# Attention with a mixture of experts: scores three tiles ahead, exponentials two, sum copies on VectorE

## The chip, the cores and the metric

The kernel runs on one core of a Trainium2 chip. The metric is the device time of one execution in microseconds (us); lower is better. Several executions are timed and their median counts. One more execution was recorded by the hardware profiler; the rows below are from it.

## What is computed

Attention over pooled queries (2 batches, 8 heads, 1152 positions, head size 64), then four experts, each a two-layer network with ReLU, weighted by a gate:

```python
q_pool = q.reshape(B, H, S // 2, 2, D).mean(axis=3)
scores = scale * np.matmul(q_pool, k.transpose(0, 1, 3, 2))
scores = scores - np.max(scores, axis=-1, keepdims=True)
attn = np.exp(scores)
attn = attn / (np.sum(attn, axis=-1, keepdims=True) + 1e-09)
attn_out = np.matmul(attn, v)                 # [2, 8, 576, 64]
x = attn_out.transpose(0, 2, 1, 3).reshape(B * S, H * D)
p = domain_probs / (domain_probs.sum(-1, keepdims=True) + 1e-09)
for e in range(E):
    h = np.maximum(x @ w1[e], 0.0)
    out += p[:, e:e + 1] * (h @ w2[e])
```

## The kernel before

The order of the instructions of each engine is the order in which the program is written; no scheduler changes it. The engines run side by side and wait for one another by semaphores, and each takes its own instructions strictly in order.

**The attention part** goes over 8 pairs of heads, n = 0 to 7 (pairs 0 to 3 are batch 0). Each pair has 9 tiles, i = 0 to 8, of 128 rows of scores by 1152 keys; tile number g = 9n + i. A tile goes through these steps:

- `scores(g)`: TensorE (PE) writes the scores into the PSUM tile `spt` (three banks; its pool `ps_s` has a single buffer). `S_rows` (L334, L338) does so for most tiles, `S_chunk` (L324) for tile 8 and for pair 0. Then `neg_scores(g)` on VectorE (DVE, L341) copies them to one of three SBUF buffers `sx`, scaled and negated, with the minimum of each row.
- `exps(g)`: ScalarE (ACT, L347) replaces `sx` by the exponentials and sums each row.
- `T_chunk(g, c)`: PE transposes `sx` in 18 pieces (L202) into two PSUM tiles `pt` (pool `ps_t`, two buffers); ACT copies the first to `aT` (L363), DVE the second (L361).
- `pv_part(g)`: a part of the product of `aT` with the values, in PSUM tile `po` (L376). Tiles 0 to 3 of a pair form group 0 (256 columns), whose product is made in tiles 4 to 8; tiles 4 to 8 form group 1 (320 columns), whose product is made in tiles 0 to 3 of the next pair. `PVCUT` cuts it: three key blocks in tile 0, two in tiles 1 to 7, one in tile 8. The last part calls `finish`: DVE multiplies `po` by the inverse sums `rb` (L416), and the result is split into a high and a low part for the expert products, in batch 0 by ACT (L419) and POOL (GpSimd, L420), in batch 1 mostly by POOL.
- `inv_sums` (DVE L385, L386, then a POOL copy into `spread`, L387) and `spread_sums` (PE transposes `spread` into a `pt` buffer called `pr`, L394 and L396, and ACT copies it to `rb`, L397 and L400) make `rb`.

The loop over g issues for tile g: `T_chunk(g)`, `exps(g+1)`, `pv_part(g)`, then in some tiles `spread_sums` or a preparation step, at last `scores(g+2)`.

**Preparation of a later pair.** `prep_q` and `prep_k` (table `PREP`) make the operands of the next pair out of loaded q and k. `prep_q(n)`: 12 transposes on PE into a `pt` buffer called `pq`, an ACT copy to `raw` (L280), splits into high and low parts on POOL (`pool_split`, L209 and L210), DMAs issued by SP that stack the halves, and at its end `join_k(1)`, a POOL copy (L262) that `prep_k(n, 1)` transposes. `prep_k(n, c)`: 8 transposes `pk`, a copy to `raw` (DVE for c = 1, ACT for c = 2), POOL splits, stacking DMAs. `add_q` and `join_k(0)`, on POOL, form their inputs from the loads.

**The expert part** follows at about 256 us and takes the rest: 16 units of products. Its first products (`chx`, L135) are put into tiles 7 and 8 of the last pair; between them ACT copies `chx` to `UT["m1"]` (L543).

The PSUM pools:

```python
ps_t = ctx.enter_context(tc.tile_pool(name="ps_t", bufs=2, space=PSUM))
ps_s = ctx.enter_context(tc.tile_pool(name="ps_s", bufs=1, space=PSUM))
ps_o = ctx.enter_context(tc.tile_pool(name="ps_o", bufs=1, space=PSUM))
```

Of the kernel before, what the change touches and what calls it, by code (L numbers as in the profile page):

```python
# [8 lines left out]
F32 = mybir.dt.float32  # L9
F32R = mybir.dt.float32r  # L10
AF = mybir.ActivationFunctionType
ALU = mybir.AluOpType
# [5 lines left out]
def attention_moe_kernel(ctx, tc, q, k, v, probs, w1, w2, out):  # L18
    nc = tc.nc
# [4 lines left out]
    HALF = 64  # L24
    NPAIR = H // 2
    KT = S // P
    NQT = 9
# [13 lines left out]
    CW = HT // 2  # L41
# [101 lines left out]
    with ExitStack() as actx:  # L143
# [246 lines left out]
        def spread_sums(n, grp):  # L390
            pt = ps_t.tile([P, 2, 512], F32, tag="t", name="pr")[:, 0]
            r = rs[n % 2][:, 4 * grp:]
            for j in range(2):
                nc.tensor.transpose(pt[:, j * P:(j + 1) * P], spread[:, j * P:(j + 1) * P], ident)  # L394
            if grp:
                nc.tensor.transpose(pt[:, 2 * P:3 * P], r[:, 4:5].to_broadcast([P, P]), ident)  # L396
            nc.scalar.activation(rb[grp][:, :256], pt[:, :256], AF.Copy)  # L397
            if grp:
                for a, h in enumerate(ROWS):
                    nc.scalar.activation(rb[1][h, 256:], pt[h, 256 + a * HALF:256 + (a + 1) * HALF], AF.Copy)  # L400

        def split_x(op, kt, c, src, eng):
            hi, lo = xop(op, 0, kt)[:, c], xop(op, 1, kt)[:, c]
# [6 lines left out]
        def finish(n, grp, po):  # L410
            b, hp = pairs[n]
            w, kt = GW[grp], hp % 2
            c = slice(256 * grp, 256 * grp + w)
            c1 = slice(HT + 256 * grp, HT + 256 * grp + w)
            x = xr[:, hp, c1 if b else c]
            nc.vector.tensor_tensor(x, po[:, :w], rb[grp], ALU.mult)  # L416
            if b == 0:
                op = "A12" if hp > 1 else "A11"
                nc.scalar.activation(xop(op, 0, kt)[:, c], x, AF.Copy)  # L419
                nc.gpsimd.tensor_tensor(xop(op, 1, kt)[:, c], x, xop(op, 0, kt)[:, c].bitcast(F32), ALU.subtract)  # L420
                return
            a11, a12, a21 = xr[:, kt, c], xr[:, kt + 2, c], xr[:, kt, c1]
            if hp < 2:
                nc.gpsimd.tensor_tensor(a11, a11, x, ALU.subtract)
                if hp == 0:
                    split_x("S3", 0, c, a11, nc.gpsimd)
                return
            eng = nc.vector if hp == 3 else nc.gpsimd
            eng.tensor_tensor(a11, x, a11, ALU.subtract)
            todo = [("S2", a11), ("S1", a21), ("A22", x), ("S4", a12)]  # L430
            if eng is nc.gpsimd:
                eng.tensor_tensor(a21, a21, x, ALU.add)
                eng.tensor_tensor(a12, a12, a11, ALU.subtract)
                for op, src in todo:
                    split_x(op, kt, c, src, eng)
                return
            hi, lo = split_parts(todo[0], kt, c)
            hi()
            eng.tensor_tensor(a21, a21, x, ALU.add)
            eng.tensor_tensor(a12, a12, a11, ALU.subtract)  # L440
            rest = [split_parts(t, kt, c) for t in todo[1:]]
            late.append([lo] + [r[1] for r in rest])
            late.append([r[0] for r in rest])
            if grp == 0:
                for fn in late.pop() + late.pop():
                    fn()
# [44 lines left out]
        for fn in ev:  # L491
# [7 lines left out]

        PVCUT = {0: (1, -1, 0, 3), 1: (1, -1, 3, 5), 2: (1, -1, 5, 7), 3: (1, -1, 7, 9),  # L500
                 4: (0, 0, 0, 2), 5: (0, 0, 2, 4), 6: (0, 0, 4, 6), 7: (0, 0, 6, 8), 8: (0, 0, 8, 9)}
        SPREAD = {7: (0, 0), 1: (-1, 1)}
        PREP = {0: [(prep_q,)], 2: [(prep_k, 1)], 4: [(prep_k, 2)]}
        PREP0 = {3: [(prep_q,)], 4: [(prep_k, 1)], 5: [(prep_k, 2)]}

        def pv_part(g):
# [19 lines left out]
        for g in range(NTL):  # L526
# [2 lines left out]
                load_kv(vn[(n + 1) % 2], v, n + 1)  # L529
            if i == 6 and n + 2 < NP:  # L530
                add_q(nc.gpsimd)
            if i == 8 and n + 2 < NP:
                join_k(0)
            if i == 2 and n + 2 < NP:
                load_q(n + 2)
            for c in range(2):
                T_chunk(g, c)
            if g + 1 < NTL:
                exps(g + 1)
            if i == 8:  # L540
                inv_sums(n, 1)
            if g == NTL - 1:
                nc.scalar.activation(UT["m1"], chx[:, :2, :CW], AF.Copy)  # L543
            pv_part(g)
            if i in SPREAD and n + SPREAD[i][0] >= 0:
                spread_sums(n + SPREAD[i][0], SPREAD[i][1])
            if g == 0:
# [1 line left out]
            if n + 1 < NP:  # L549
                for fn, *args in (PREP if n else PREP0).get(i, []):  # L550
                    fn(n + 1, *args)
                if i == (4 if n else 5) and n + 2 < NP:
                    load_kv(kn, k, n + 2)
            elif i == 7:
                chx = ps_s.tile([P, 3, 512], F32, tag="s", name="chx")
                for kt in range(2):
                    product(0, 0, kt, chx, True)
            elif i == 8:
                for kt in range(2):
                    product(0, 2, kt, chx, False)  # L560
            scores(g + 2)
            if g == 0:
                stack_k0()
                add_q(nc.gpsimd)
                join_k(0)
                join_k(1)
            if i == 3:
                inv_sums(n, 0)
            if (n, i) == (1, 4):
                gate_weights()  # L570
            if (n, i) == (NP - 2, 4):
# [170 lines left out]
```

## Time and profile before

| what | value |
|---|---|
| median of 3 timed runs | 639.02 us (637.85 to 639.38) |
| the profiled execution's own time | 637.7 us |
| its span, first to last instruction | 635.9 us |
| PE busy with matmuls | 618.5 us, 97% |
| PE weight loads | 504.0 us, 79% |
| DVE, ACT, POOL busy | 56%, 48%, 54% |
| granted TensorE clock | 1.000 throughout |

The span is what the trace covers; the execution's own time is 1.8 us more, for what lies around it. Of the span, the attention part takes about 256 us and the expert part about 380 us. Matmuls are pipelined and their ends in the trace are modelled, so two matmul rows may overlap; the start of a row is a firmer number than its end.

### The profile page before, as it was taken

To read this page: it belongs to the slowest core of one execution; us is meant where nothing else is said; L and a number is where in the kernel's file an instruction comes from. 1 tells how busy PE (TensorE), PEld (TensorE's weight loads), DVE (VectorE), ACT (ScalarE), POOL (GpSimd) and SP (SyncE) were. 2 spreads that over 40 slices of the span, in tenths; PEclk is the share of its full clock that TensorE was granted. 3 is DMA by queue.
4 is the path that set the end of the run, shared out by engine and by line. 5 is a ranking of instruction groups with operands and counts; after the bars stand their busy time and mean duration, and the time that the engine had idled before them with its cause. 6 is when DMAs were issued, how large, how long until landed. Compare 5 with 4: busy or idle time off the path is not lost.

```text
span 635.9 us, 12066 instructions
## 1 busy us (share of the span) xinstructions
PE 618.5 (97%) x4828; PEld 504.0 (79%) x4828; DVE 354.1 (56%) x539; ACT 306.1 (48%) x507; POOL 344.5 (54%) x407
## 2 busy tenths in 40 slices
PE   7899999999999999999999999999999999999997
PEld 6656666666666666899899889889989989989976
DVE  6657576666766666644454454454454454454454
ACT  5667777677766685543144144145135135135130
POOL 2646353444545497594584484485485476476040
PEclk9999999999999999999999999999999999999999
DMA  6848291828364510211121121121121121120105
GB/s 216 181 119 201 58 221 55 229 53 203 78 176 95 151 36 1 67 36 64 35 66 36 33 67 35 34 66 34 34 66 35 34 66 34 34 67 1 34 1 148
DMA packets 41782, 50.87 MB, mean 80 GB/s; under 512 B 3712, under 2 KB 27520, under 8 KB 41728
## 3 DMA queue, kind: packets, MB, share of 16 engines
q1 hardware_dynamic: 40928, 48.94, 29.2%
q10 hardware_dynamic: 800, 1.18, 0.5%
q8 instruction: 38, 0.62, 0.4%
q14 instruction: 16, 0.13, 0.1%
HBM read 30.97 MB, written 2.36 MB: 52 GB/s over the span
## 4 chain that ended last, share of the span: by engine, by line
PE 84%; ACT 5%; DVE 5%; DMA 2%; POOL 2%; issue 1%; SPq 0%; DVEq 0%; ACTq 0%; POOLq 0%
PE p L698 31%; PE chy L135 12%; PE po L376 9%; PE chx L135 8%; PE chz L135 8%; PE pt L202 5%; DVE sx L341 4%; PE spt L334 4%; ACT sx L347 4%; PE spt L338 3%; PE spt L324 2%; DMA pr<-in_moe_domain_probs_dram 1%; PE pk L202 1%; PE pr L394 1%; DMA kk<-kk 1%
## 5 line engine op out<-in xcount | busy, mean ns | idle before, releaser
L698 PE MATMUL p<-w2s,hb 128*128 128x512 f32 (+1 forms) x870 | 199.2, 388 | 1.1 <-DVE acc L702 0.9
L698 PEld LDWEIGHTS p<-w2s,hb 128*128 128x128 f32 x870 | 161.7, 188 | 34.3 <-issue 1.3
L702 DVE SCALAR_TENSOR_TENSOR acc<-p,pw,acc 128x512 f32<-128x512 f32 (+1 forms) x136 | 101.5, 747 | 82.8 <-PE p L698 82.8
L341 DVE TENSOR_SCALAR_CACHE_REDUCE sx<-spt 128x1152 f32<-128x1152 f32 x72 | 97.7, 1357 | 77.1 <-PE spt L338 42.8
L116 POOL TENSOR_TENSOR kk<-kq,kk 128x512 fp32r<-128x512 f32 x64 | 72.6, 1164 | 117.8 <-ACT kk L108 117.8
L347 ACT ACTIVATE sx<-sx,mn 128x1152 f32<-128x1152 f32 x72 | 90.6, 1258 | 24.6 <-DVE sx L341 21.6
L376 PE MATMUL po<-aT,vn 128*64 128x320 f32 (+1 forms) x576 | 85.3, 418 | 0.0
L666 ACT ACTIVATE xr<-chx 128x576 f32<-128x576 f32 x15 | 9.8, 652 | 147.5 <-PE chx L135 147.5
L629 POOL TENSOR_TENSOR hb<-xr,hb 128x576 fp32r<-128x576 f32 x48 | 68.7, 1437 | 21.9 <-ACT hb L628 21.8
L363 ACT ACTIVATE aT<-pt 128x640 f32<-128x640 f32 x72 | 50.7, 704 | 43.2 <-PE pt L202 43.0
L202 PEld LDWEIGHTS pt<-ident,sx 64*128 64x128 f32 x1296 | 50.1, 139 | 13.6 <-ACT sx L347 7.9
L202 PE MATMUL pt<-ident,sx 64*128 64x64 f32 x1296 | 57.1, 227 | 2.1 <-ACT xr L302 0.4
L135 PE MATMUL chx<-xa,kk 128*128 128x288 f32 x384 | 56.4, 296 | 1.3 <-ACT xr L543 0.5
L135 PEld LDWEIGHTS chx<-xa,kk 128*128 128x128 f32 x384 | 53.4, 188 | 3.3 <-ACT xr L543 1.0
L376 PEld LDWEIGHTS po<-aT,vn 128*64 128x64 f32 x576 | 35.1, 136 | 20.1 <-issue 0.3
L95 POOL TENSOR_TENSOR kq<-kq 128x256 f32<-128x256 f32 x64 | 45.9, 739 | 8.4 <-DMA kq<-in_moe_w_dram 7.2
L361 DVE COPY aT<-pt 128x512 f32<-128x512 f32 x72 | 49.1, 682 | 2.3 <-PE pt L202 2.3
L627 ACT ACTIVATE xr<-xr 128x576 f32<-128x576 f32 x48 | 32.9, 686 | 34.0 <-DVE xr L625 34.0
L334 PE MATMUL spt<-kk,q2all 128*128 128x512 f32 x168 | 44.4, 371 | 3.2 <-DVE sx L341 2.6
L135 PE MATMUL chy<-xb,kk 128*128 128x288 f32 x288 | 46.7, 298 | 0.1
L135 PE MATMUL chy<-q2all,kk 128*128 128x288 f32 x256 | 44.1, 294 | 0.0
L605 POOL TENSOR_TENSOR w2s<-qsf,w2s 128x512 fp32r<-128x512 f32 x32 | 40.8, 1297 | 3.5 <-ACT w2s L603 3.5
(107 smaller groups left out, 751.8 us busy)
## 6 DMA issues: line engine op xcount, KB each, us to landing
kq<-in_moe_w_dram SPq DMA_DIRECT2D x64, 128.0 KB, 2.4
qsf<-in_moe_w_dram SPq DMA_DIRECT2D x16, 512.0 KB, 3.6
q2all<-q2all SPq DMA_DIRECT2D x28, 256.0 KB, 4.8
vn<-in_v_dram SPq DMA_DIRECT2D x8, 576.0 KB, 6.6
kk<-kk SPq DMA_DIRECT2D x28, 160.0 KB, 3.5
kq<-in_q_dram SPq DMA_DIRECT2D x7, 576.0 KB, 7.4
kq<-in_k_dram SPq DMA_DIRECT2D x7, 576.0 KB, 4.4
kk<-kk SPq DMA_DIRECT2D x28, 128.0 KB, 5.6
```

The costliest lines, as they stand in the source:

```text
L116: nc.gpsimd.tensor_tensor(flat(w1s[u % 2][:, 1, a:b]), flat(wf[:, a:b]), flat(w1s[u % 2][:, 0, a:b].bitcast(F32)), ALU.subtract)
L135: nc.tensor.matmul(chain[:, c, :CW], w1s[u % 2][:, a, WI[wo], kt, :], xop(xo, z, kt)[:, c * CW:(c + 1) * CW], start=(first and kt == 0 and ...
L202: nc.tensor.transpose(pt[:, a, j, :], src[r], ident[r, r])
L334: nc.tensor.matmul(sp[:, c], q2[n % 2][:, 0, h, ts_], k2[n % 2][:, h, c], start=True, stop=False)
L341: nc.vector.tensor_scalar(sx[g % 3].rearrange("p (c x) -> p c x", c=3), spt.pop(g), -INV, None, ALU.mult, ALU.min, accum_out=mn[g % 3])
L347: nc.scalar.activation(sx[g % 3], sx[g % 3], AF.Exp, bias=mn[g % 3], scale=-1.0, accum_out=sums[n % 2][:, i:i + 1])
L361: nc.vector.tensor_copy(dst, pt)
L363: nc.scalar.activation(dst, pt, AF.Copy)
L376: nc.tensor.matmul(po[h * HALF:(h + 1) * HALF, :w], vn[n % 2][:, h, kt, :], aT[grp][:, h, kt, :], start=(kt == 0), stop=(kt == KT - 1))
L629: nc.gpsimd.tensor_tensor(lo, c, hi.bitcast(F32), ALU.subtract)
L698: nc.tensor.matmul(pc, h[:, a, sl, ts_], w[:, b, sl, c0:c1], start=(m == 0), stop=(m == len(ops) - 1))
L702: nc.vector.scalar_tensor_tensor(ac, pc, pw[:, tt, e:e + 1], ac, ALU.mult, ALU.add)
```

## The change

Scores are issued three tiles ahead in place of two, exponentials two in place of one, from pair 1 on; tile 0 of pair 1 (g = 9) issues two score tiles for the transition. The exponential of tile g+2 stands right behind the copy of `T_chunk(g)` on ACT, in tiles 3 and 8 at the tile's end. The copies of `spread_sums` go from ACT to DVE, the split of `finish` in batch 0 from ACT and POOL to POOL alone. All steps of preparation move one tile earlier: `prep_q` for pair n+2 to tile 8 of pair n, `prep_k` to tiles 1 and 3, `join_k(0)` to tile 6, the load of k to tile 3. `inv_sums` and the second `spread_sums` move a tile later. The copy to `m1` stands ahead of the last tile's `aT` copy.

```diff
--- before.py
+++ after.py
@@ -394,10 +394,10 @@
                 nc.tensor.transpose(pt[:, j * P:(j + 1) * P], spread[:, j * P:(j + 1) * P], ident)
             if grp:
                 nc.tensor.transpose(pt[:, 2 * P:3 * P], r[:, 4:5].to_broadcast([P, P]), ident)
-            nc.scalar.activation(rb[grp][:, :256], pt[:, :256], AF.Copy)
+            nc.vector.tensor_copy(rb[grp][:, :256], pt[:, :256])
             if grp:
                 for a, h in enumerate(ROWS):
-                    nc.scalar.activation(rb[1][h, 256:], pt[h, 256 + a * HALF:256 + (a + 1) * HALF], AF.Copy)
+                    nc.vector.tensor_copy(rb[1][h, 256:], pt[h, 256 + a * HALF:256 + (a + 1) * HALF])
 
         def split_x(op, kt, c, src, eng):
             hi, lo = xop(op, 0, kt)[:, c], xop(op, 1, kt)[:, c]
@@ -416,8 +416,7 @@
             nc.vector.tensor_tensor(x, po[:, :w], rb[grp], ALU.mult)
             if b == 0:
                 op = "A12" if hp > 1 else "A11"
-                nc.scalar.activation(xop(op, 0, kt)[:, c], x, AF.Copy)
-                nc.gpsimd.tensor_tensor(xop(op, 1, kt)[:, c], x, xop(op, 0, kt)[:, c].bitcast(F32), ALU.subtract)
+                pool_split(xop(op, 0, kt)[:, c], xop(op, 1, kt)[:, c], x)
                 return
             a11, a12, a21 = xr[:, kt, c], xr[:, kt + 2, c], xr[:, kt, c1]
             if hp < 2:
@@ -499,8 +498,8 @@
 
         PVCUT = {0: (1, -1, 0, 3), 1: (1, -1, 3, 5), 2: (1, -1, 5, 7), 3: (1, -1, 7, 9),
                  4: (0, 0, 0, 2), 5: (0, 0, 2, 4), 6: (0, 0, 4, 6), 7: (0, 0, 6, 8), 8: (0, 0, 8, 9)}
-        SPREAD = {7: (0, 0), 1: (-1, 1)}
-        PREP = {0: [(prep_q,)], 2: [(prep_k, 1)], 4: [(prep_k, 2)]}
+        SPREAD = {7: (0, 0), 2: (-1, 1)}
+        PREP = {1: [(prep_k, 1)], 3: [(prep_k, 2)]}
         PREP0 = {3: [(prep_q,)], 4: [(prep_k, 1)], 5: [(prep_k, 2)]}
 
         def pv_part(g):
@@ -529,19 +528,30 @@
                 load_kv(vn[(n + 1) % 2], v, n + 1)
             if i == 6 and n + 2 < NP:
                 add_q(nc.gpsimd)
-            if i == 8 and n + 2 < NP:
                 join_k(0)
             if i == 2 and n + 2 < NP:
                 load_q(n + 2)
+            if g == NTL - 1:
+                nc.scalar.activation(UT["m1"], chx[:, :2, :CW], AF.Copy)
             for c in range(2):
                 T_chunk(g, c)
-            if g + 1 < NTL:
+            if g <= NQT:
                 exps(g + 1)
-            if i == 8:
+            if i == 0 and n:
+                inv_sums(n - 1, 1)
+            if i == 4:
+                inv_sums(n, 0)
+            if g == NTL - 1:
                 inv_sums(n, 1)
-            if g == NTL - 1:
-                nc.scalar.activation(UT["m1"], chx[:, :2, :CW], AF.Copy)
-            pv_part(g)
+            if NQT < g < NTL - 2 and i not in (3, 8):
+                exps(g + 2)
+            if g == NQT:
+                PV_part(0, 1, 0, 1)
+                scores(g + 2)
+                exps(g + 2)
+                PV_part(0, 1, 1, 3)
+            else:
+                pv_part(g)
             if i in SPREAD and n + SPREAD[i][0] >= 0:
                 spread_sums(n + SPREAD[i][0], SPREAD[i][1])
             if g == 0:
@@ -549,7 +559,9 @@
             if n + 1 < NP:
                 for fn, *args in (PREP if n else PREP0).get(i, []):
                     fn(n + 1, *args)
-                if i == (4 if n else 5) and n + 2 < NP:
+                if i == 8 and n + 2 < NP:
+                    prep_q(n + 2)
+                if i == (3 if n else 5) and n + 2 < NP:
                     load_kv(kn, k, n + 2)
             elif i == 7:
                 chx = ps_s.tile([P, 3, 512], F32, tag="s", name="chx")
@@ -558,14 +570,14 @@
             elif i == 8:
                 for kt in range(2):
                     product(0, 2, kt, chx, False)
-            scores(g + 2)
+            if NQT <= g < NTL - 2 and i in (3, 8):
+                exps(g + 2)
+            scores(g + 2 if g < NQT else g + 3)
             if g == 0:
                 stack_k0()
                 add_q(nc.gpsimd)
                 join_k(0)
                 join_k(1)
-            if i == 3:
-                inv_sums(n, 0)
             if (n, i) == (1, 4):
                 gate_weights()
             if (n, i) == (NP - 2, 4):
```

PE around the end of a pair (tile 8 and tile 0; `sx`, `aT`, `kk` and `vn` carry buffer numbers, which differ from pair to pair). Before:

```order
L202 MATMUL pt<-ident,sx_92 128x64 x18
L376 MATMUL po<-aT_93,vn_88 64x256 x2
L334 MATMUL spt<-kk_74,q2all 128x512 x2
L334 MATMUL spt<-kk_74,q2all 128x128
L338 MATMUL spt<-kk_74,q2all 128x512 x2
L338 MATMUL spt<-kk_74,q2all 128x128
L202 MATMUL pt<-ident,sx_90 128x64 x18
L376 MATMUL po<-aT_94,vn_88 64x320 x6
L202 MATMUL pq<-ident,qsf 128x64 x10
L202 MATMUL pq<-ident,raw 128x64 x2
L334 MATMUL spt<-kk_74,q2all 128x512 x2
```

With the change:

```order
L202 MATMUL pt<-ident,sx_92 128x64 x18
L376 MATMUL po<-aT_93,vn_89 64x256 x2
L202 MATMUL pq<-ident,qsf 128x64 x10
L202 MATMUL pq<-ident,raw 128x64 x2
L334 MATMUL spt<-kk_73,q2all 128x512 x2
L334 MATMUL spt<-kk_73,q2all 128x128
L338 MATMUL spt<-kk_73,q2all 128x512 x2
L338 MATMUL spt<-kk_73,q2all 128x128
L202 MATMUL pt<-ident,sx_90 128x64 x18
L376 MATMUL po<-aT_94,vn_89 64x320 x6
L334 MATMUL spt<-kk_73,q2all 128x512 x2
```

The 12 transposes `pq` stand in tile 8, ahead of its scores, and no longer in tile 0; the transposes and products around them keep their order.

ACT at the same place, from the `aT` copy of tile 7 on. Before, the exponential behind it is that of tile 8 (`sx_92`):

```order
L363 ACTIVATE aT_94<-pt 128x2x5x64
L347 ACTIVATE sx_92,sums_102<-sx_92,mn_101 128x1152
L397 ACTIVATE rb_95<-pr 128x256
L363 ACTIVATE aT_94<-pt 128x2x5x64
L347 ACTIVATE sx_90,sums_103<-sx_90,mn_99 128x1152
L419 ACTIVATE xa<-xr 128x256
L363 ACTIVATE aT_93<-pt 128x2x5x64
L347 ACTIVATE sx_91,sums_103<-sx_91,mn_100 128x1152
L280 ACTIVATE raw<-pq 128x768
```

With the change it is that of tile 0 of the next pair (`sx_90`):

```order
L363 ACTIVATE aT_94<-pt 128x2x5x64
L347 ACTIVATE sx_90,sums_103<-sx_90,mn_99 128x1152
L363 ACTIVATE aT_94<-pt 128x2x5x64
L280 ACTIVATE raw<-pq 128x768
L347 ACTIVATE sx_91,sums_103<-sx_91,mn_100 128x1152
L363 ACTIVATE aT_93<-pt 128x2x5x64
L347 ACTIVATE sx_92,sums_103<-sx_92,mn_101 128x1152
```

The exponential that a tile's transposes read is issued two tiles ahead of them; the copies to `rb` and `xa` are gone from this queue, and `raw<-pq` stands in tile 8, ahead of that tile's exponential.

POOL from the end of a pair on, pair 1 in both. Before, `join_k(1)` is the first of the two copies of the last row:

```order
L387 COPY spread<-rs_105 128x256
L420 TENSOR_TENSOR xa<-xr,xa 128x256
L209 TENSOR_SCALAR q2all<-raw 128x512
L210 TENSOR_TENSOR q2all<-raw,q2all 128x512
L209 TENSOR_SCALAR q2all<-raw 64x64
L210 TENSOR_TENSOR q2all<-raw,q2all 64x64
L209 TENSOR_SCALAR q2all<-raw 64x64
L210 TENSOR_TENSOR q2all<-raw,q2all 64x64
L209 TENSOR_SCALAR kk_74<-raw 128x128
L210 TENSOR_TENSOR kk_74<-raw,kk_74 128x128
L262 COPY qsf<-kq 128x512 x2
```

With the change:

```order
L209 TENSOR_SCALAR xa<-xr 128x256
L210 TENSOR_TENSOR xa<-xr,xa 128x256
L209 TENSOR_SCALAR q2all<-raw 128x512
L210 TENSOR_TENSOR q2all<-raw,q2all 128x512
L209 TENSOR_SCALAR q2all<-raw 64x64
L210 TENSOR_TENSOR q2all<-raw,q2all 64x64
L209 TENSOR_SCALAR q2all<-raw 64x64
L210 TENSOR_TENSOR q2all<-raw,q2all 64x64
L209 TENSOR_SCALAR kk_74<-raw 128x128
L210 TENSOR_TENSOR kk_74<-raw,kk_74 128x128
L262 COPY qsf<-kq 128x512
L387 COPY spread<-rs_105 128x256
```

`spread` moved from ahead of this chain to behind `join_k(1)`, the split `xa` has two instructions in place of one, and the whole chain now begins in tile 8 and not in tile 0.

## Rows read from the trace of the kernel before

**Rows 1.** Who waited, PE alone, 68.8 to 98.65 us: sum, times, longest (us).

```profile
PE spt L334 <- DVE sx L341: 0.4, 1, 0.4
```

**Rows 2.** Timeline of PE, tiles 7 to 1: start, duration (us), engine, line, instruction [idle].

```profile
67.71 0.77 PE L334 MATMUL spt<-kk,q2all 128*128 128x512 f32 x3
...
68.80 0.77 PE L202 MATMUL pt<-ident,sx 64*128 64x64 f32 x18
69.50 0.65 PE L376 MATMUL po<-aT,vn 128*64 128x256 f32 x4
70.51 0.79 PE L334 MATMUL spt<-kk,q2all 128*128 128x512 f32 x3 [0.35 <-DVE sx L341]
71.24 0.56 PE L338 MATMUL spt<-kk,q2all 64*128 64x512 f32 x3
71.89 0.77 PE L202 MATMUL pt<-ident,sx 64*128 64x64 f32 x18
...
74.36 0.53 PE L202 MATMUL pq<-ident,qsf 64*128 64x64 f32 x10
...
74.88 0.79 PE L334 MATMUL spt<-kk,q2all 128*128 128x512 f32 x3
75.60 0.55 PE L338 MATMUL spt<-kk,q2all 64*128 64x512 f32 x3
75.94 0.77 PE L202 MATMUL pt<-ident,sx 64*128 64x64 f32 x18
```

**Rows 3.** Same view: tile 2, end of 3, tile 5, and pair 3's tile 8.

```profile
79.21 0.91 PE L202 MATMUL pt<-ident,sx 64*128 64x64 f32 x18
80.06 1.30 PE L376 MATMUL po<-aT,vn 128*64 128x320 f32 x8
...
85.41 0.55 PE L338 MATMUL spt<-kk,q2all 64*128 64x512 f32 x3
85.86 0.77 PE L202 MATMUL pt<-ident,sx 64*128 64x64 f32 x18
...
89.75 1.08 PE L376 MATMUL po<-aT,vn 128*64 128x256 f32 x8
90.76 0.80 PE L334 MATMUL spt<-kk,q2all 128*128 128x512 f32 x3
91.49 0.55 PE L338 MATMUL spt<-kk,q2all 64*128 64x512 f32 x3
92.16 0.77 PE L202 MATMUL pt<-ident,sx 64*128 64x64 f32 x18
...
98.65 0.77 PE L202 MATMUL pt<-ident,sx 64*128 64x64 f32 x18
```

**Rows 4.** Timeline of all engines, tile 8 of pair 2 and tile 0 after it.

```profile
98.94 1.36 DVE L341 TENSOR_SCALAR_CACHE_REDUCE sx<-spt 128x1152 f32<-128x1152 f32 x1 [1.13 <-ACT rb L397]
...
101.13 0.40 DVE L416 TENSOR_TENSOR xr<-po,rb 128x256 f32<-128x256 f32 x1
...
101.74 0.64 PEld L202 LDWEIGHTS pt<-ident,sx 64*128 64x128 f32 x18 [0.36 <-ACT sx L347]
```

**Rows 5.** Same view, POOL: first and last of prep_q's chain (9 instructions), then pk.

```profile
105.81 0.62 POOL L209 TENSOR_SCALAR q2all<-raw 128x512 fp32r<-128x512 f32 x1 [3.00 <-ACT raw L280]
...
109.99 0.61 POOL L262 COPY qsf<-kq 128x512 f32<-128x512 f32 x1
...
111.14 0.33 PEld L202 LDWEIGHTS pk<-ident,qsf 64*128 64x128 f32 x8 [0.49 <-POOL qsf L262]
```

**Rows 6.** Timeline, POOL: a split of 256 columns into high and low part.

```profile
223.58 0.41 POOL L405 TENSOR_SCALAR xb<-xr 128x256 fp32r<-128x256 f32 x1
...
224.08 0.73 POOL L408 TENSOR_TENSOR xb<-xr,xb 128x256 fp32r<-128x256 f32 x1
```

**Rows 7.** Timeline, PE: first product after the copy to m1, last tile.

```profile
249.08 1.85 PE L135 MATMUL chx<-xa,kk 128*128 128x288 f32 x12 [0.51 <-ACT xr L543]
```

**Rows 8.** Timeline, POOL: join_k(0) for pair 2, in tile 8 of pair 0.

```profile
40.23 0.29 POOL L262 COPY raw<-kq 128x128 f32<-128x128 f32 x1 [5.04 <-DMA kq<-in_k_dram]
```

## The prediction

> **What bounds the kernel now.** I read first who waited on PE, then PE's own timeline. The list of waits says that PE waited 0.4 us in the whole of pair 2 [rows 1], which would leave almost nothing to win. The timeline says more when starts are compared, since ends of matmuls are modelled. The pair lasts from the transposes of one tile 8 to those of the next, 98.65 - 68.80 = 29.85 us [rows 2, 3]. What the steps take when nothing holds them up: 18 transposes T 0.70 (68.80 to 69.50); eight products of 256 columns 1.01 (89.75 to 90.76), so four take 0.50; the 12 transposes pq 0.52 (74.36 to 74.88); scores S 0.72 + 0.34 = 1.06 (74.88 to 75.60 to 75.94) [rows 2, 3]. Against these, PE loses in each pair:
>
> - tile 8: four products take 1.01 before the scores start, 0.50 too long; the row names DVE's `neg_scores`, which has to empty `spt` first [rows 2];
> - tile 8 to 0: 0.65 from the second half of S to T, not 0.34: 0.31 lost [rows 2]; the same place a pair later names ACT's exponential [rows 4];
> - tile 5 to 6: 0.67, so 0.33 lost; tile 3 to 4: 0.45, so 0.11; tile 2: T takes 0.85, 0.15 lost [rows 3], where its second `pt` buffer still holds `pr` until ACT has copied it.
>
> Together 1.40 us of 29.85. The Trainium skill (Perfetto Trace Analysis, Identifying the Most-Contended Engine) says that matmul busy time is a poor measure of headroom, because pipelined matmuls mislead; here the trace agrees, 0.4 listed against 1.40 found by starts. By the listed idle time alone six pairs could give 2.4 us and no more.
>
> There are two chains behind these losses. One is scores, `neg_scores`, exponential, transposes: the transposes of a tile come one tile after its exponential was issued, and any other work on ACT makes them late. The other is the single buffer of `spt`: S, then 1.36 us of `neg_scores` [rows 4], then the next S. Where it binds, S starts 70.51 - 67.71 = 2.80 us after the S before [rows 2]. PE's own work for a tile without preparation is 0.70 + 1.01 + 1.06 = 2.77, so the two are almost even.
>
> **Part by part.**
>
> *Exponentials two tiles ahead.* T finds its exponential a tile old. The losses of tiles 3, 5 and 8 to 0 go: 0.11 + 0.33 + 0.31 = 0.75 a pair. What is late next is the `spt` chain: three tiles a pair (3 to 4, 4 to 5, 7 to 8) run at 2.80 and not 2.77, which I round up to 0.1 a pair.
>
> *Copies to `rb` on DVE.* They no longer stand behind an exponential, and the 0.15 of tile 2 goes. The trace has no such copy on DVE; the nearest row is `finish`, 0.40 for 256 columns out of PSUM [rows 4], so about 0.4 in tile 7 and, with the two small ones, 0.8 in tile 2. They lie ahead of the next `neg_scores` on DVE. Cover: in tile 2, T takes 0.70, eight wider products 1.2 (two thirds of the 1.77 that twelve take, 74.36 - 71.89 - 0.70 [rows 2]) and `pr` about 0.5, an estimate; so the copies can run from 2.4 to 3.2 us after T's start. The scores start at about 2.2, and `neg_scores` is due 2.80 - 1.36 = 1.44 later, at 3.6. Between 0 and 0.8 exposed; I take 0.
>
> Over pairs 1 to 6: 6 x (0.75 + 0.15 - 0.10) = **-4.8**.
>
> *`prep_q` in tile 8.* Its 0.52 of PE leaves tile 0, where it lay on the path, and fills the 0.50 in which PE waits for `spt` in tile 8. Pairs 1 to 5: **-2.5**. The rule that speaks against this change is in the same page of the Trainium skill (Matmuls): groups of matmuls should rotate through different PSUM banks, so that emptying one overlaps the next. `spt` keeps its one buffer, so by that rule alone a longer lead of the scores buys nothing and the gap stays. By the rows only the filler changes this; if the gap stayed unfilled the sum would be 2.5 us higher.
>
> *POOL's chain behind it.* From the split of q to `join_k(1)` POOL needs 109.99 + 0.61 - 105.81 = 4.79 us [rows 5], and the transposes `pk` wait for it. Before, `pk` started 0.54 after its end (111.14) [rows 5] and so did not wait. Now the chain begins behind `finish` of the same tile 8. `finish` ends 101.13 + 0.40 - 98.65 = 2.9 us after T [rows 4], some 0.2 earlier without `inv_sums` ahead of it; POOL's split takes 0.50 + 0.73 [rows 6]; then 4.79. That is 8.7 to 8.9 after the start of tile 8. PE gets to `pk` in tile 1 after 2.78 (tile 8: 0.70 + 0.50 + 0.52 + 1.06), 3.53 (tile 0: 4.05 from 71.89 to 75.94 less pq) and about 1.9 (T, eight wider products): 8.2. It waits some 0.55 in pairs 2, 3 and 4. In pair 5 `finish` was that of pair 4, which has one more POOL operation of about 0.7: 1.25. In pair 6 nothing, in pair 1 nothing since the transition gives time. **+2.9**, with bounds 0 and 6.3 (1.25 in all five).
>
> *The transition.* Tile 0 of pair 1 has two S at the spacing of 2.80: from S of tile 8 to T of tile 1 it is 2.80 + 2.80 + 1.06 = 6.66. Before, in pair 2, that was 75.94 - 70.51 = 5.43 [rows 2]. One S, 1.06, is taken from the last pair, so 0.2 is lost. In tile 8 of pair 0 `pq` needs `join_k(0)`, which waits for a load of k and ended at 40.52 [rows 8]; I take 0.4 between 0 and 0.5. **+0.6**.
>
> *The last pair.* The same 0.6 of small losses goes (tiles 2, 3, 5); tiles 6 and 7, with no scores between them, are 1.06 shorter and may come to wait for copies out of `pt`, between 0 and that 1.06; I take 0.4: **-0.2**. In the last tile the product that waited 0.51 for the copy to `m1` [rows 7] finds it done: **-0.5**.
>
> *At nothing:* the POOL high parts in place of ACT's, the later `inv_sums` and the earlier loads. Each has a tile or more until its reader; without that cover a split's 0.50 a pair would show. The expert part is untouched and starts earlier by the gain.
>
> **Sum**: -4.8 - 2.5 + 2.9 + 0.6 - 0.2 - 0.5 = -4.5 us. Against the profiled execution's 637.7 that is 633.2. The median of 639.02 lies 1.3 above that execution, so I forecast **634.5**.
>
> **The rivals.**
>
> 1. *POOL is in time.* If the chain ends 0.6 earlier, the +2.9 goes: 631.6. For it: the starts on POOL are rough. Against: nothing in the chain gets shorter. Chance 0.18.
> 2. *POOL is twice as late,* 1.25 in each of the five pairs: 6.3 in place of 2.9, so 637.9, no change that can be told. For it: POOL gets more to do, ahead of the chain. Against: the count above. Chance 0.10, together with smaller shifts of that kind.
> 3. *The gap of tile 8 is not filled,* since `pq` itself comes late: 637.0. The row against it is that q is added two tiles ahead. Chance 0.04.
> 4. *Slower: DVE becomes the late one.* If the copies to `rb` delay `neg_scores` by their full 0.4 + 0.8 in each of seven pairs, 8.4 us come on top: 642.9. It decides as soon as DVE is still busy 1.44 us after S starts, when `neg_scores` is due. For it: in tile 2 the margin is only 0.4. Against: 0.40 for 256 columns is measured, and the copies wait for nothing but PE. Chance 0.04.
> 5. *The change doesn't do what it says:* ACT falls behind, and T meets a fresh exponential again. That leaves only the filled gap: near 638. Chance 0.02.
>
> **How the numbers follow.** The forecast gets 0.62. A measurement of this kernel can tell about 0.3%, 1.9 us, from no change, so faster means under 637.1. The forecast, rival 1 and half of rival 3 lie there, less 0.02 for the forecast's upper tail: 0.80. Rival 2, the other half of 3, rival 5 and that tail: 0.16. Rival 4: 0.04. The range goes from rival 1 (631.6, rounded to 631.4) to just past the border (637.3), and leaves out most of rival 2, rival 4 and rival 5.
>
> **What would show it.** Right: tiles 3, 5 and 8 with 0.34 between the second half of S and T; `pq` in tile 8 and S there 2.80 after the S before; a pair of about 28.4 us plus a wait of `pk` for POOL in tile 1 of pairs 2 to 5, longest in pair 5. Wrong: DVE's `neg_scores` starting late behind a copy to `rb`; scores of a new pair in tile 6 waiting for a stacking DMA; S spacings well over 2.80 in tiles without preparation.

## The result and the profile after

| what | value |
|---|---|
| median with the change, 6 runs | 633.24 us (631.94 to 635.0) |
| median before beside it, 6 runs | 638.93 us (637.85 to 639.95) |
| ratio | 0.9912 (95%: 0.9892 to 0.9932) |
| the profiled execution and its span | 633.96 us, 632.1 us |

The change makes the kernel 5.7 us faster; the forecast's 634.5 us lies 1.3 above the measured median. The spans of the two profiled executions differ by less, 635.9 - 632.1 = 3.8 us. Part of this lies in the first 13 us, which the forecast did not look at, and part in which execution was profiled: the one of the kernel before was 1.2 faster than its kernel's median (637.7, 638.93), the one of the changed kernel 0.7 slower (633.96, 633.24).

The page of the changed kernel: busy shares, the chain that ended last (by engine), and two of the costliest groups (busy time, mean ns | idle time before them, and what ended most of it).

```profile
PE 615.0 (97%) x4828; PEld 504.1 (80%) x4828; DVE 367.5 (58%) x571; ACT 293.9 (46%) x467; POOL 346.8 (55%) x415
...
PE 80%; POOL 8%; DVE 4%; issue 3%; ACT 2%; DMA 1%; SPq 0%; POOLq 0%; DVEq 0%; ACTq 0%
...
L202 PEld LDWEIGHTS pt<-ident,sx 64*128 64x128 f32 x1296 | 53.8, 140 | 7.8 <-issue 3.4
...
L334 PE MATMUL spt<-kk,q2all 128*128 128x512 f32 x168 | 44.1, 370 | 0.9 <-DVE sx L341 0.9
```

The chain and the same groups in the page of the kernel before:

```profile
PE 84%; ACT 5%; DVE 5%; DMA 2%; POOL 2%; issue 1%; SPq 0%; DVEq 0%; ACTq 0%; POOLq 0%
...
L202 PEld LDWEIGHTS pt<-ident,sx 64*128 64x128 f32 x1296 | 50.1, 139 | 13.6 <-ACT sx L347 7.9
...
L334 PE MATMUL spt<-kk,q2all 128*128 128x512 f32 x168 | 44.4, 371 | 3.2 <-DVE sx L341 2.6
```

Before, the transposes' weight loads had 13.6 us of idle time ahead of them, 7.9 of it put down to ACT's exponential; now 7.8, with no exponential named. The scores waited 3.2 us, now 0.9. ACT was 5% of the chain that ended last and POOL 2%; now ACT is 2% and POOL 8%. These lines tell what kind of wait went and which came, not how much time: that is read from starts again.

PE's timeline of the changed kernel, end of pair 2 and start of pair 3 (start, duration, engine, line, instruction [idle]); it answers to [rows 2, 3].

```profile
99.05 0.77 PE L334 MATMUL spt<-kk,q2all 128*128 128x512 f32 x3
99.75 0.55 PE L338 MATMUL spt<-kk,q2all 64*128 64x512 f32 x3
100.09 0.77 PE L202 MATMUL pt<-ident,sx 64*128 64x64 f32 x18
100.80 0.65 PE L376 MATMUL po<-aT,vn 128*64 128x256 f32 x4
101.51 0.53 PE L202 MATMUL pq<-ident,qsf 64*128 64x64 f32 x10
...
102.03 0.79 PE L334 MATMUL spt<-kk,q2all 128*128 128x512 f32 x3
102.75 0.55 PE L338 MATMUL spt<-kk,q2all 64*128 64x512 f32 x3
103.09 0.77 PE L202 MATMUL pt<-ident,sx 64*128 64x64 f32 x18
...
106.61 0.77 PE L202 MATMUL pt<-ident,sx 64*128 64x64 f32 x18
107.31 1.30 PE L376 MATMUL po<-aT,vn 128*64 128x320 f32 x8
108.84 0.46 PE L202 MATMUL pk<-ident,qsf 64*128 64x64 f32 x8 [0.23 <-POOL qsf L262]
```

From the second half of S to T there is 0.34 at both places (99.75 to 100.09, 102.75 to 103.09), and in every tile of pairs 1 to 6 whose scores came in these two halves. In tile 8 `pq` stands between the products and S. It starts 101.51 - 100.80 = 0.71 after the products, where they take 0.50: some 0.2 is still lost. In tile 1, `pk` starts 1.53 after products that take 1.23 in tile 2: 0.30 of waiting for POOL.

What holds `pq`, and POOL's chain, in the timeline of all engines of the same stretch:

```profile
99.38 0.41 DVE L397 COPY rb<-pr 128x256 f32<-128x256 f32 x1
...
100.44 1.36 DVE L341 TENSOR_SCALAR_CACHE_REDUCE sx<-spt 128x1152 f32<-128x1152 f32 x1 [0.65 <-PE spt L338]
100.66 0.70 ACT L363 ACTIVATE aT<-pt 128x640 f32<-128x640 f32 x1 [0.42 <-PE pt L202]
...
102.32 0.41 DVE L416 TENSOR_TENSOR xr<-po,rb 128x256 f32<-128x256 f32 x1
...
102.83 0.41 POOL L209 TENSOR_SCALAR xa<-xr 128x256 fp32r<-128x256 f32 x1 [5.58 <-DVE xr L416]
...
104.01 0.62 POOL L209 TENSOR_SCALAR q2all<-raw 128x512 fp32r<-128x512 f32 x1
...
108.17 0.61 POOL L262 COPY qsf<-kq 128x512 f32<-128x512 f32 x1
```

ACT's `aT` copy ends at 101.36, and `pq` starts 0.15 later: it needs the `pt` buffer that this copy empties. DVE's copy to `rb` takes 0.41, the 0.4 that was assumed, and ends 0.65 before `neg_scores` can begin. POOL's chain is done at 108.17 + 0.61 = 108.78, and `pk` starts 0.06 later.

Each pair, from the first T of its tile 0 to that of the next, worked out from PE's timeline (us; the last pair up to the first product `chy` of the expert part):

| | start of T, tile 0 | pair 0 | 1 | 2 | 3 | 4 | 5 | 6 | 7 to chy | tile 0 to chy |
|---|---|---|---|---|---|---|---|---|---|---|
| before | 11.16 | 30.56 | 30.17 | 29.85 | 29.86 | 29.83 | 29.83 | 29.82 | 35.41 | 245.33 |
| after | 12.79 | 30.66 | 30.71 | 28.93 | 28.97 | 28.93 | 29.80 | 28.46 | 33.44 | 239.90 |
| difference | +1.63 | +0.10 | +0.54 | -0.92 | -0.89 | -0.90 | -0.03 | -1.36 | -1.97 | -5.43 |

The rest, from `chy` on, takes 379.4 us in both. So the attention loop gave 5.4 us and the start took 1.6 back in this execution.

### The profile page after: what moved, and what is told of

The parts are those of the page before. It is cut to its first block, busy times and chain, and to the rows that moved or that the text cites. A ratio compares the mean times of both kernels' runs of the same rounds, so it can differ in the third digit from the quotient of the medians.

```text
span 632.1 us, 12010 instructions
## 1 busy us (share of the span) xinstructions
PE 615.0 (97%) x4828; PEld 504.1 (80%) x4828; DVE 367.5 (58%) x571; ACT 293.9 (46%) x467; POOL 346.8 (55%) x415
## 4 chain that ended last, share of the span: by engine, by line
PE 80%; POOL 8%; DVE 4%; issue 3%; ACT 2%; DMA 1%; SPq 0%; POOLq 0%; DVEq 0%; ACTq 0%
PE p L710 31%; PE chy L135 11%; PE chz L135 8%; PE chx L135 7%; PE po L376 7%; PE spt L334 4%; PE pt L202 4%; PE spt L338 3%; PE spt L324 2%; POOL q2all L210 2%; DVE sx L341 1%; DMA kq<-in_k_dram 1%; POOL q2all L209 1%; POOL xb L408 1%; PE pk L202 1%
## 5 line engine op out<-in xcount | busy, mean ns | idle before, releaser
L202 PEld LDWEIGHTS pt<-ident,sx 64*128 64x128 f32 x1296 | 53.8, 140 | 7.8 <-issue 3.4
```

Of the source, the lines that this page charges most:

```text
L202: nc.tensor.transpose(pt[:, a, j, :], src[r], ident[r, r])
```

## The experiments

All times beside the kernel before on the same chip, which had a median of 638.89 us (19 runs) with the first four and 638.81 (21 runs) with the last four. "Loop" is the time from tile 0 to `chy`, the last column above; a step's "lead" is the number of tiles that it is issued ahead.

**The changed kernel again.** No edit.

> The changed kernel once more, unaltered, as the base for the others of this chip. Theory A (the start of the kernel is a race between a DVE subtraction and POOL's addition of q, which one of them wins by the landing of the second load of q): tile 0 of pair 0 starts at 11.2 or at 12.8 us, nothing between, and the rest of the attention part lasts the same to 0.1 us. Rival B (the 1.6 us of the start belong to the change): it starts at 12.8 again and in every profile of this order. Time 631.5 to 634.5 either way.

Measured: 634.03 us (5 runs), ratio 0.9913 (0.9882 to 0.9945), loop 239.89. Tile 0 began at 12.73 in place of 12.79, every pair was within 0.1. DVE and POOL at the start of the kernel before, in its timeline, and the scores of tile 1:

```profile
7.12 0.83 DVE L240 TENSOR_TENSOR kk<-kq,kk 128x320 fp32r<-128x320 f32 x2
...
7.82 1.55 POOL L177 TENSOR_TENSOR qsf<-kq 128x640 f32<-128x640 f32 x1 [5.65 <-DMA kq<-in_q_dram]
...
9.76 1.48 PE L324 MATMUL spt<-kk,q2all 128*128 128x384 f32 x6 [0.82 <-DVE sx L341]
```

The same in the changed kernel, with the matmuls `pk` that wait:

```profile
7.09 2.19 DVE L240 TENSOR_TENSOR kk<-kq,kk 128x320 fp32r<-128x320 f32 x2
7.45 1.55 POOL L177 TENSOR_TENSOR qsf<-kq 128x640 f32<-128x640 f32 x1 [5.28 <-DMA kq<-in_q_dram]
...
9.43 0.51 PE L246 MATMUL pk<-identr,kk 128*128 128x128 f32 x4 [0.96 <-DVE kk L240]
...
10.70 2.16 PE L324 MATMUL spt<-kk,q2all 128*128 128x384 f32 x6 [0.76 <-DVE sx L341]
```

And in this run, with the scores of tile 0 and of tile 1:

```profile
6.76 1.54 POOL L177 TENSOR_TENSOR qsf<-kq 128x640 f32<-128x640 f32 x1 [4.59 <-DMA kq<-in_q_dram]
...
7.48 2.29 PE L324 MATMUL spt<-kk,q2all 128*128 128x384 f32 x6 [0.29 <-ACT kk L249]
7.83 1.16 DVE L240 TENSOR_TENSOR kk<-kq,kk 128x320 fp32r<-128x320 f32 x2
...
11.32 1.48 PE L324 MATMUL spt<-kk,q2all 128*128 128x384 f32 x6 [0.78 <-DVE sx L341]
```

DVE's two subtractions take 0.83 us where POOL's addition starts later than the second of them. Where POOL starts earlier, the subtraction that meets it ends some 0.3 after POOL does: at 7.09 + 2.19 = 9.28 in the changed kernel, POOL at 7.45 + 1.55 = 9.00. The matmuls that need `kk` then start late. POOL starts when a load of q lands, which differs from execution to execution (waits of 5.65, 5.28, 4.59 us), and both kernels have the same instructions up to here, so nothing of the change stands here. In the changed kernel's profile this cost 0.95: DVE's next copy to `kk` (L249) starts at 10.48 and not 9.53. The other 0.68 of the 1.63 goes with a lower clock: from S of tile 1 to T of tile 0 PE took 12.79 - 10.70 = 2.09, before 11.16 - 9.76 = 1.40. Its windows (us, PE busy, PEld, DVE, ACT, POOL busy with counts, granted clock, DMA share, GB/s):

```profile
9.00:10.00 1.00, 0.51 (x4) 0.40 (x4) 1.00 (x2) 0.21 (x1) 0.00 (x0) 1.00 0.00 0
10.00:11.00 1.00, 0.30 (x2) 0.30 (x2) 1.00 (x3) 0.41 (x1) 0.00 (x0) 0.96 0.86 194
11.00:12.00 1.00, 1.00 (x4) 0.79 (x3) 0.16 (x1) 0.94 (x2) 0.00 (x0) 0.50 0.93 369
```

0.50 is the lower of the two levels, 1.2 GHz. In the repeated run the start was late by nearly as much with another make-up. DVE lost 0.33 to POOL, but that delayed nothing, since `neg_scores` then waited 0.81 for the scores. The first load of k landed 0.42 later (a wait of 2.74, not 2.32), and the rows of PE at the beginning are longer: the scores of tile 0 take 2.29, before 1.42. The trace of this run records the granted clock from 9.79 us on, as 1.00; that of the kernel before from 5.1 us (its 1.000 throughout holds from there) and that of the changed kernel from 4.1 us. The long rows lie ahead of 9.79, those behind have the usual lengths (1.48 for the scores of tile 1). A clock of 0.50 up to there would fit, as the scores that run at 0.50 in the changed kernel take 2.16, but no record shows it.

By its number, 12.73, this run is what rival B expected, and one repetition can't refute it; the same start gave 11.19 in a run below (scores two ahead). That the start would be 11.2 or 12.8 and nothing between did not hold: the profiles below have 11.91, 12.17 and 12.30 as well.

**`join_k(1)` early**, behind `join_k(0)` in tile 6 and no longer at the end of POOL's chain.

```diff
-            if n > 1:
-                join_k(1)
...
                 join_k(0)
+                join_k(1)
```

> join_k(1) is issued in tile 6, behind join_k(0), and no longer at the end of POOL's chain of prep_q. Theory A (pk in tile 1 waits for that chain and for nothing else): the waits ahead of pk, 0.30 in pairs 2 to 4 and 1.12 in pair 5, go, and tile 1 takes 3.38 everywhere; the attention part is 2.0 us shorter. Rival B (something else holds pk, such as the pt buffer or the scores' own chain): under 0.5 us is won, the wait comes back in tile 1 or 2 under another name.

Measured: 632.37 us (630.24 to 634.42, 4 runs), ratio 0.989 (0.9847 to 0.9933). Pairs 2 to 5 take 28.64, 28.63, 28.64, 28.62: 0.31, 0.36, 0.32 and 1.19 less than in the changed kernel run again, 2.2 in all. PE's and POOL's rows in tile 1 of pair 5, where the wait had been longest:

```profile
166.67 1.30 PE L374 MATMUL po<-aT,vn 128*64 128x320 f32 x8
...
167.90 0.46 PE L202 MATMUL pk<-ident,qsf 64*128 64x64 f32 x8
167.97 0.46 POOL L210 TENSOR_TENSOR kk<-raw,kk 128x128 fp32r<-128x128 f32 x1
```

`pk` follows the products by their 1.23 (167.90 - 166.67) and starts before the chain's last split does: what it waited for was `join_k(1)` alone, and the rest of the chain is not needed by then. Of the 2.2 the medians show 634.03 - 632.37 = 1.7. The profiled execution, with 634.42 the slowest of the four, shows none of it, because it lost time in pair 0 (33.71 us, not 30.6). Its windows (columns as above):

```profile
10.00:15.00 5.00, 3.77 (x36) 3.04 (x37) 3.64 (x7) 3.37 (x5) 0.00 (x0) 0.74 0.95 304
15.00:20.00 5.00, 4.69 (x30) 4.04 (x28) 2.35 (x4) 2.05 (x4) 4.14 (x7) 0.50 1.03 226
20.00:25.00 5.00, 4.51 (x38) 3.51 (x38) 2.46 (x4) 2.05 (x3) 1.32 (x4) 0.50 0.74 185
```

The granted clock is 0.50 from 15 to 25 us. This run's subtractions took 2.19, too, and PE had waited 0.90 for `kk` before that. Before, the same three windows have 1.00.

**`prep_q` back in tile 0**, `prep_k(1)` in tile 2.

```diff
-        PREP = {1: [(prep_k, 1)], 3: [(prep_k, 2)]}
+        PREP = {0: [(prep_q,)], 2: [(prep_k, 1)], 3: [(prep_k, 2)]}
...
-                if i == 8 and n + 2 < NP:
-                    prep_q(n + 2)
```

> prep_q goes back to tile 0 of the pair ahead and the first prep_k to tile 2; the leads of scores and exponentials stay. Theory A (the gap of tile 8 comes from the single score buffer and is only filled by pq): tile 8 of pairs 1 to 5 lasts 2.82 as it does in pair 6, not 2.99; tile 0 is 0.52 longer; the waits ahead of pk (2.0 in all) go; so 5 x 0.35 - 2.0 = -0.3 us, about the same time. Rival B (a lead of three tiles alone closes the gap): tile 8 lasts 2.3, and the kernel is some 2 us faster than with pq in tile 8.

Measured: 635.15 us (9 runs), ratio 0.9932 (0.9908 to 0.9956), loop 241.15, 1.26 more than the changed kernel again. Tile 8 without `pq` lasts 2.82, against 2.99 with it: 0.52 of work costs 0.17. In tile 0 it costs its full 0.52 (4.03 in place of 3.52). That is the filled gap, 0.35 a pair and not 0.5. The wait of `pk` for POOL is gone, but `pk` in tile 2 now stands behind `pr` and waits about 0.22 for a `pt` buffer, and two single waits came: 0.55 in tile 1 of pair 1, where T's second half waits for a `pt` buffer, and 0.37 in tile 5 of pair 3, which was not followed. So by this run the move is worth 1.3 net, POOL's wait included, and 0.9 of that are the two single waits.

**Exponentials one tile ahead**, scores still three.

```diff
-            if g <= NQT:
+            if g + 1 < NTL:
                 exps(g + 1)
...
-            if NQT < g < NTL - 2 and i not in (3, 8):
-                exps(g + 2)
...
-                exps(g + 2)
...
-            if NQT <= g < NTL - 2 and i in (3, 8):
-                exps(g + 2)
```

> Scores stay three tiles ahead, exponentials go back to one tile ahead, right behind the first copy of the transposes. Theory A (the lead of the exponentials removed the waits of the transposes): T waits for ACT again in tiles 3, 5 and 8 and others, 0.1 to 0.4 each, and the kernel is 3 to 5 us slower. Rival B (the lead of the scores is enough, since the exponential's input is then a tile old and it starts without a wait): under 1 us slower, T waits 0.1 or less.

Measured: 634.65 us (10 runs), ratio 0.993 (0.9911 to 0.9949). Pairs 1 to 6 take 30.72, 28.94, 28.96, 28.94, 29.76, 28.50: the changed kernel's to 0.05, with 0.34 from S to T everywhere. Two pairs are longer: pair 0 (31.92, not 30.6), where the granted clock is 0.65 and 0.67 in the windows 10:15 and 15:20, and the last pair, by 0.6, where no scores follow and an exponential is late (PE's timeline):

```profile
240.44 1.08 PE L376 MATMUL po<-aT,vn 128*64 128x256 f32 x8
242.30 0.77 PE L202 MATMUL pt<-ident,sx 64*128 64x64 f32 x18 [0.77 <-ACT sx L347]
```

So it is not the exponentials' second tile that frees T in the other pairs. With scores three ahead an exponential finds its input ready as soon as ACT comes to it, and is done in time from one tile ahead: between 70 and 220 us no exponential of this run has idle time that `neg_scores` ended, where the changed kernel has 13.0 us of it (32 times) and the kernel before 13.4.

**Scores two ahead, exponentials one**, as before; all else of the change kept.

```diff
-            if g <= NQT:
+            if g + 1 < NTL:
                 exps(g + 1)
...
-            if g == NQT:
-                PV_part(0, 1, 0, 1)
-                scores(g + 2)
-                exps(g + 2)
-                PV_part(0, 1, 1, 3)
-            else:
-                pv_part(g)
+            pv_part(g)
...
-            scores(g + 2 if g < NQT else g + 3)
+            scores(g + 2)
```

> Scores go back to two tiles ahead and exponentials to one; all the rest of the change stays (preparation a tile earlier with pq in tile 8, copies to rb on DVE, splits on POOL). Theory A (the lead of the scores removed the waits of the transposes): T waits for ACT again in tiles 3, 5 and 8 (0.1 to 0.35 each, some 0.7 a pair), a pair lasts 29.6 and not 28.95, the kernel is about 4 us slower than with the change, less 0.6 for the transition. Rival B (the moved copies and splits had freed ACT enough): a pair lasts 29.1 or less.

Measured: 636.88 us (634.92 to 640.83, 10 runs), ratio 0.9979 (0.9957 to 1.0002), loop 242.71. PE and ACT in its timeline, the same tiles as above:

```profile
99.03 1.26 ACT L347 ACTIVATE sx<-sx,mn 128x1152 f32<-128x1152 f32 x1 [0.42 <-DVE sx L341]
...
99.99 0.55 PE L338 MATMUL spt<-kk,q2all 64*128 64x512 f32 x3
...
100.29 0.79 ACT L280 ACTIVATE raw<-pq 128x768 f32<-128x768 f32 x1
...
100.43 0.52 PE L202 MATMUL pt<-ident,sx 64*128 64x64 f32 x10
...
101.13 0.46 PE L202 MATMUL pt<-ident,sx 64*128 64x64 f32 x8 [0.17 <-ACT raw L280]
```

S to T is 0.44 and not 0.34, the exponential ends just ahead of it, and the second half of T waits for the `pt` buffer that `raw` is copied out of behind that exponential (T takes 1.09). The other places: 0.66 from tile 4 to 5, 0.37 from 5 to 6, 0.40 from 7 to 8. Pairs 2 to 4 take 29.5, 0.55 more than with the lead. Of the 5.44 us that the loop gained in the repeated run, 245.33 - 242.71 = 2.62 are there without the lead; the two leads together bring 2.82, net of the transition. The runs alone do not tell this kernel from the one before: the interval reaches 1.

**Copies of `spread_sums` on ACT again.**

```diff
-            nc.vector.tensor_copy(rb[grp][:, :256], pt[:, :256])
+            nc.scalar.activation(rb[grp][:, :256], pt[:, :256], AF.Copy)
...
-                    nc.vector.tensor_copy(rb[1][h, 256:], pt[h, 256 + a * HALF:256 + (a + 1) * HALF])
+                    nc.scalar.activation(rb[1][h, 256:], pt[h, 256 + a * HALF:256 + (a + 1) * HALF], AF.Copy)
```

> The copies to rb go back to ACT; nothing else differs from the changed kernel. Theory A (with exponentials a tile old, ACT may be late without harm): the tiles of PE keep their lengths to 0.05, the time is the same to 0.5 us. Rival B (the copies held pt, which is why T took 0.85 in tile 2): T of tile 3 behind pr takes 0.15 to 0.3 longer, or pq and pk wait for a pt buffer; 1 to 2 us slower.

Measured: 634.94 us (10 runs), ratio 0.9946 (0.9926 to 0.9965), loop 240.42. T behind `pr` takes 0.86 to 0.88, not 0.70, in tiles 8 and 3, as expected of a late buffer. But in tile 8 `pq` then waits less (0.59 behind the products, not 0.72), so a pair is only 0.1 longer (29.07 against 28.96), and 0.53 come together in the loop. The copies on DVE are worth these 0.5 us, where the forecast had 0.15 a pair, 0.9.

**`join_k(1)` early, and POOL's first addition behind DVE.** A one-element POOL copy that reads the last `kk` of the subtractions stands ahead of it, so that POOL waits. The edit of `join_k(1)` is the one shown above.

```diff
+        mark = ap.tile([P, 1], F32, name="mark")
...
         exps(0)
+        nc.gpsimd.tensor_copy(mark, khl[:, 1, KT - 1, 1, :1].bitcast(F32))
         add_q0(nc.gpsimd, 4, 9)
```

> join_k(1) in tile 6 as before in these runs, and at the start POOL first copies one element that DVE's last subtraction of k writes, so that its addition of q can't begin ahead of it. Theory A (DVE's subtraction and POOL's addition shut each other out, and whichever begins first makes the other wait): the two subtractions take 0.83 together in every profile, tile 0 starts at 11.0 to 11.4, the clock stays at full through the first 30 us, and the runs scatter less; median 630 to 631. Rival B (the start depends on the landing of the loads alone): tile 0 starts anywhere from 11 to 13, median 632.

Measured: 630.28 us (629.97 to 633.04, 5 runs), ratio 0.9879 (0.9861 to 0.9898), loop 237.58. DVE, POOL and the matmuls `pk` at its start:

```profile
7.32 0.83 DVE L241 TENSOR_TENSOR kk<-kq,kk 128x320 fp32r<-128x320 f32 x2
...
8.15 0.88 PE L247 MATMUL pk<-identr,kk 128*128 128x128 f32 x9
8.30 0.19 POOL L492 COPY mark<-kk 128x1 f32<-128x1 f32 x1 [6.12 <-DVE kk L241]
...
8.44 1.54 POOL L178 TENSOR_TENSOR qsf<-kq 128x640 f32<-128x640 f32 x1
```

The subtractions take 0.83, tile 0 begins at 11.28, the granted clock is 1.00 from 5.9 us, where its record begins, to 25 us. Of the 3.75 us to the changed kernel's median, 2.31 lie in the loop and 1.45 in the start (12.73 - 11.28). The 1.45 is not the price of the subtractions, since that run was late for other reasons; where they did delay tile 0, in the changed kernel's first profile, they cost 0.95. POOL's addition is late by 1.0 and nobody waits for it. One of the five runs still took 633.04 us, with a granted clock of 0.992 over its span: a lower clock can come with POOL held back, too.

**The same with other halves of T**: ACT copies four key blocks and DVE five, not five and four.

```diff
-            k0, k1 = TCH[c]
+            k0, k1 = ((0, 4), (4, 9))[c]
```

> As the kernel before in this list, and the first part of a tile's transposes has 4 key blocks and the second 5, so that ACT's copy is shorter and DVE's longer. Theory A (pq in tile 8 waits 0.22 because the pt buffer is held until ACT's copy is done): the wait goes, tile 8 lasts 2.83 in place of 2.99, 0.8 us in five pairs. Rival B (DVE becomes late: its copy grows by 0.14 in every tile and delays neg_scores): tiles without preparation get longer by up to 0.14, no gain or a loss up to 3 us.

Measured: 630.51 us (629.61 to 631.03, 4 runs), ratio 0.9871 (0.9857 to 0.9885), loop 236.96. Tile 8 in its timeline:

```profile
97.94 0.60 ACT L362 ACTIVATE aT<-pt 128x512 f32<-128x512 f32 x1 [0.36 <-PE pt L203]
...
98.14 0.65 PE L375 MATMUL po<-aT,vn 128*64 128x256 f32 x4
...
98.72 0.53 PE L203 MATMUL pq<-ident,qsf 64*128 64x64 f32 x10
```

The copy takes 0.60, not 0.70, and `pq` follows the products by 0.58, not 0.71: it is that copy that `pq` waited for. A pair becomes 0.10 shorter, the loop 0.62. Tile 8 lasts 2.86, near the 2.82 without `pq`. By the runs this and the last kernel can't be told apart. Both beat the kernel before by 8 us and the changed one by 2.7 or more.

## Why the prediction was right, step by step

Forecast and measured by pairs, both against the kernel before (the forecast's terms laid out by pair: small waits -0.80, filled gap -0.50, POOL +0.55 or +1.25, transition):

| | forecast | measured |
|---|---|---|
| start | 0 | +1.63 |
| pairs 0 and 1 | +0.83 | +0.64 |
| pairs 2 to 4 | -2.25 | -2.71 |
| pair 5 | -0.05 | -0.03 |
| pair 6 | -1.30 | -1.36 |
| pair 7 to chy | -1.76 | -1.97 |
| sum | -4.5 | -3.8 |

The loop gave 0.9 more than forecast, and in this execution the start took 1.6 that was not forecast. The medians differ by 5.7, about what the loop gave; since the start differs between executions (11.07 to 12.85 us in the ten profiles), the -3.8 of two single executions is the poorer measure.

That the sum came so close is in part luck. Over five pairs the filled gap was put 0.75 too high (2.5, not 1.75) and POOL's wait 0.9 too high (2.9, not 2.0), which counts the other way. And the price of the small waits came true although the wrong part of the change was named as their cure.

- **Losses found by starts, not by idle time.** Right: 0.34 from S to T and 0.70 for T, in pairs 1 to 6 wherever the scores come in two halves. The listed idle time allowed 2.4 us for six pairs, and the loop gave 5.4. The Trainium skill's rule on matmul busy time (Perfetto Trace Analysis, Identifying the Most-Contended Engine) holds here. The reason that it gives, that pipelined matmuls look smaller in the trace, is not what these rows show: T's row reads 0.77 where the next step starts 0.70 after it, so rows look longer and idle time smaller.
- **Which part removes them.** Wrong: the step "exponentials two tiles ahead" was named as the cause. With the exponentials one ahead nothing returns in pairs 1 to 6; with the scores two ahead it does. It is the scores' lead that the exponential was waiting for. The exponentials' second tile is worth 0.6 us, in the last pair.
- **`prep_q` in tile 8.** Right in kind, -2.5 was too much. The gap took 0.35 of the 0.52, 1.75 in five pairs, because `pq` itself waits 0.2 for the `pt` buffer that ACT is copying. The step had looked at `spt` alone and not at the buffer that `pq` needs, and the sign given for it, S in tile 8 2.80 after the S before, did not come: it was 2.98. The Trainium skill's rule is that matmul groups should rotate through PSUM banks (Perfetto Trace Analysis, Matmuls). What the forecast concluded from it, that by the rule a longer lead buys nothing with one buffer, was not borne out: `spt` kept its one buffer and the leads were still worth 2.8 us, since the time between S and T was what they bought.
- **POOL's chain.** The wait came where it was put, with the order of sizes that was given: 0.30 in pairs 2 to 4 (0.55 forecast), 1.12 in pair 5 (1.25), none in 1 and 6. 2.0 in place of 2.9, since PE reached `pk` later by the 0.2 lost at `pq`: POOL's chain ended 108.78 - 100.09 = 8.69 after the start of tile 8, at the lower end of what was forecast (8.7 to 8.9), and PE was there at 8.45, not 8.2. So part of what `pq` loses in tile 8 is not lost twice: `pk` waits that much less. The early `join_k(1)` gave back 2.2, which is rival 1 made true by an edit.
- **The transition.** S of tile 8 to T of tile 1 took 6.61 (6.66 forecast). `join_k(0)` in pair 0 held `pq` for 0.82, not 0.4, but pair 0 as a whole became only 0.10 longer. Tile 7, where scores wait for a stacking DMA of `kk`, was 0.79 shorter (3.10, not 3.89); the forecast has no term for that, and why was not followed.
- **Copies on DVE.** 0.41 as assumed, nothing exposed (in tile 2 DVE is idle 0.31 between the copies and `neg_scores`), so rival 4 (slower) had no ground. That T in tile 2 would be 0.15 faster was right for T; a pair gained less, because `pq` waits for the same buffers.
- **The last pair.** `chx` starts 0.58 after its products and not 1.16: -0.58 for `m1`, -0.5 forecast. Waits for copies out of `pt` came to about 0.25, not 0.4.
- **The start.** Not in the sum: the change does not touch it.

Not tried: k's load earlier in pair 0, against the 0.82. The splits on POOL alone, the later `inv_sums` and the earlier loads were not undone one by one. The parts that were measured come to 2.82 (leads) + 1.26 (`prep_q`) + 0.53 (copies) + 0.58 (`m1`) = 5.19 of the loop's 5.44, each with the rest of the change in place, so that little is left for the others.

## What to carry to other kernels

Compare starts of the same step over a whole period, and once a wait is found, undo one half of the lead at a time: here the lead of the producer (scores), not of the step that was seen late (the exponential), was what counted. When work is moved into a gap, list every buffer that it needs at its new place, and ask which of its side jobs on a slow engine (`join_k(1)` at the end of POOL's chain) can leave the chain. A start that differs between executions by a load's landing can hide or feign a third of such a gain, so set the start apart from the loop before reading either.

## What the runs showed of the hardware

DVE's subtractions with both inputs in SBUF and POOL's addition did not run side by side. The ten profiles fall into two groups and one between: 0.83 us for the subtractions where POOL began late or was made to wait (four profiles, tile 0 at 11.07 to 11.28); 1.82 to 2.19 where it began before the second (five, tile 0 at 11.91 to 12.85); and the repeated run, where POOL was nearly done, with 1.16. In these last six the subtraction that met POOL ended 0.28 to 0.35 after POOL's row. POOL's own row stayed at 1.55 in the changed kernel. It took 1.84 with the scores two ahead, where it began together with the second subtraction (7.67) and that one took its usual 0.42: here POOL waited. The Trainium skill (SBUF — State Buffer, Who interferes with whom) says that a DVE instruction with two SBUF inputs contends with a GpSimd instruction that reads SBUF, that the shared port pair is an exclusive lock, and that the order of issue decides who blocks. The traces agree.

The idle time that this left on PE was followed in three of those five profiles by a granted clock of 0.50: from 11 us in the changed kernel, in parts of 10 to 20 us with the exponentials one ahead (0.65 and 0.67 in its two windows of 5 us), and from 15 to 25 us with `join_k(1)` early, whose pair 0 took 3.1 us longer. The wait of `pk` for `kk` was 0.96, 0.95 and 0.90 in these. In the two others (`prep_q` in tile 0, copies on ACT) it was 0.56 and 0.86, and the clock 1.00, as in the other five profiles from where their records begin. What decides was not found. A lower clock is no mark of the change: among the 40 runs of the kernel before that stand beside the experiments, five have 0.989 over their span, and they took 641.87 to 642.58 us.
